# A new order for the opening of a sparse-attention and gated feed-forward kernel

## The chip, the core and the metric

The kernel runs as one program on one core of a Trainium2 chip. The time is that of the whole program on the device, in microseconds. Three runs of the kernel before gave 633.43, 633.52 and 633.88 us; the median is 633.52 us. A separate profiled execution gives the trace that is read here.

## The reference

Attention comes first. For each of 4 batches and 8 heads there are 768 positions of 64 numbers. A query sees the keys closer than 16 positions and 24 summaries of the whole sequence, one for every 32 positions: the largest key of a block (by element) with the mean of its values. Then each token's 8 heads are joined to 512 numbers and pass a feed-forward layer with a gate.

```python
block, window = (32, 16)
k_sum = k.reshape(B, H, nb, block, D).max(axis=3)
v_sum = v.reshape(B, H, nb, block, D).mean(axis=3)
scores_l = scale * np.matmul(q, k.transpose(0, 1, 3, 2))
mask_l = np.abs(pos[:, None] - pos[None, :]) < window
scores_s = scale * np.einsum('bhsd,bhnd->bhsn', q, k_sum) + np.log(block)
a = softmax over [scores_l where mask_l, scores_s]      # in words
attn = np.matmul(a, np.concatenate([v, v_sum], axis=2))
h = x @ w_in            # 3072 x 512 by 512 x 2048
return (h * np.cos(h)) @ w_out
```

## The kernel before

The 3072 tokens are cut into 8 blocks of 384. In a block the heads go in four pairs, called a, b, c and d; `a0` is pair a of block 0, `b1` pair b of block 1. The feed-forward width of 2048 is cut into 16 slices of 128 (`w0` to `w15`), and a *step* (`s0` to `s127`) is one slice of one block: four groups of three matmuls up, the gate, and nine matmuls down. Steps 0 to 5 and 22 to 31 belong to block 0, steps 6 to 21 to block 1. Each float32 operand of a step is split into a high and a low part, so three products stand for one.

Nothing is scheduled by a compiler: a table `ORDER` of 2098 short words is read from left to right, and each word records the instructions of one operation. Each engine then runs its instructions in the order in which they were recorded, and a semaphore holds an instruction back until what it reads is there. So a word that waits holds back everything behind it on its engine. A word names whose it is, what is done, and then PSUM banks or buffers and the engine: `a` is ScalarE (ACT), `v` VectorE (DVE), `p` GpSimd (POOL). The words that matter below:

- `k`, `q`, `v`, `l`: loads, all issued by SyncE's queue (SP). `v1_0.l` is the first of eight loads with block-wise V of batch 1; all eight land in one buffer, `kn` (line 246), so the next can start only when the last one is summed.
- `tk`, `tq`: TensorE turns K and Q (lines 516 and 503); `ck`, `cq` copy them out of PSUM; `ks` takes the largest key of each block (line 535); `ms` and `sc` put mask and scores into PSUM (lines 554 and 579); `mx` is the maximum (line 597), `ex` the exponential (line 614), `iv` the inverse sum (lines 624 and 627).
- `nm` multiplies the weights by it on POOL (line 630), `tp` turns them (line 639), `cp` copies them out, `va` multiplies by the values (line 683), and `xh` and `xl` write the result as high part and rest (lines 372 and 376).
- `m` copies the means of V under a pair's values, on POOL (line 372, `<-early`); in batch 0 the means come from `vm` and `ve`.
- `v1_0.s` sums such a load of V: as one reduction on DVE (line 261), or on POOL by halving (lines 251 and 267 or 270).
- A weight slice is made by `ab` and `sh` on ACT, `fb` on DVE (line 416), then `hi` and `lo` (lines 372 and 376).
- `u` is a quarter of a step's products up (line 738), `up` all of them (line 726); `tu`, `re`, `si`, `ga` the gate (the last is line 758 and frees the bank); `dh` and `dl` the products down (line 786).
- `h0.w` to `h7.w` are eight matmuls with no use for the result, put between the first operations (line 930).

The loop that reads the table (lines 1001 to 1006):

```python
    with tc.manual_schedule(engines=everything):
        prepare()
        for token in ORDER.split():
            who, what, *args = token.split(".")
            one = whose[who]
            getattr(one, does[type(one)][what])(*(int(a) if a.isdigit() else eng_of[a] for a in args))
```

Of the kernel before, what the change touches and what calls it, by code (L numbers as in the profile page):

```python
# [37 lines left out]
c1.m.p d1.ms.4.2 c0.xh.v d1.sc c0.xl d0.va.0 b1.nm d1.mx.1 b0.cp.0.a b0.cp.1.v a1.tp.0.7 w2.ab.1 c1.iv a1.tp.1.6 c1.nm
s1.u.0.3 w2.sh d0.xh.v d1.ex.3 d0.xl b0.va.1 b0.xh.v s0.u.0.5 b0.xl v1_2.s.p s0.u.2 s1.u.2 s1.u.3 a1.cp.0.v c1.tp.1.7
s1.u.1 s0.u.3 w2.fb w2.hi.v a1.cp.1.a d1.iv d1.v c1.v c1.tp.0.2 s0.u.1 s1.tu.0 w4.l.6 w5.ab.0 a1.va.4 s0.tu.1 w2.lo.v  # L40
w5.sh v1_3.l s0.re d1.nm s1.re s2.u.0.6 s2.u.2 s2.u.3 c1.cp.0.a d1.tp.1.1 c1.cp.1.v c1.va.2 d1.tp.0.0 w3.l.7 s0.si
w5.fb w5.hi.v d1.cp.1.a b1.tp.0.7 w5.lo.v s1.si s1.ga s0.ga d1.cp.0.a b1.v s2.u.1 d1.va.1 b1.tp.1.0 s5.u.0.5 a1.xh.a
c1.xh.a w8.l.0 a1.xl s1.hi.0.a s0.hi.1.a d1.xh.v d1.xl s1.lo.0.v s0.lo.1.v w4.ab.1 b1.cp.1.a w4.sh v1_3.s.v s5.u.2
s2.tu.0 s5.u.3 s2.re b1.m.p v1_4.l s5.u.1 w4.fb s0.dh.1.0.3 s2.si s0.dl s2.ga s2.hi.1.v s2.lo.1.p w3.ab.0 b1.cp.0.v
c1.xl w4.hi.a s1.dh s1.dl s2.dh s2.dl w4.lo.v b1.va.4 w3.sh s4.u.0.6 s4.u.2 w9.l.1 b1.xh.a w3.fb w3.hi.v b1.xl s4.u.3
w3.lo.p s4.u.1 w8.ab.1 s5.tu.1 w7.l.7 s6.up.4 v1_4.s.0.v s4.tu.0 s4.re w8.sh v1_5.l s4.si s5.re s3.u.0.2 s5.si w9.ab.0
w8.fb w10.l.2 s4.ga s4.hi.0.v s11.up.7 s4.lo.0.p s5.ga w9.sh s5.hi.1.a w9.fb s3.u.2 s3.u.3 s3.u.1 w8.hi.a s3.tu.0
s5.lo.1.v w9.hi.a w6.l.6 s6.tu.1 s10.up.6 w8.lo.p a2.v a2.m s3.re s6.re s5.dh s3.si s3.ga s3.hi.1.v w7.ab.1 w9.lo.v
s4.dl s3.lo.0.p s4.dh s3.dh v1_5.s.v w7.sh w10.ab.0 s3.dl s5.dl w7.fb w7.hi.v s6.si s6.ga s8.up.2 s6.hi.0.v w10.sh
s11.tu.0 s6.lo.0.v w10.fb s5.ta.0.a s10.tu.1 w10.hi.a w10.lo.p w7.lo.v s9.up.4 s11.re s10.re s5.ta.1.v s11.si s10.si  # L50
w6.ab.1 s7.up.1 s11.ga v1_6.l s10.ga w12.l.7 v1_6.s.v s10.hi.1.a w6.sh s10.lo.1.v v1_7.l s6.dh.5.7.6 w6.fb w12.ab.0
s11.hi.0.a s6.dl s11.lo.0.v w6.hi.a s5.ta.2.v s7.tu.1 s8.tu.0 s7.re s10.dh s11.dh s10.dl v1_7.s.v s11.dl w12.sh s7.si
s8.re w13.l.6 s7.ga s16.up.0 s8.si s8.ga s8.hi.1.a s15.up.1 w12.fb s7.hi.0.a s14.up.2 a2.k s5.st.0 w6.lo.v w12.hi.a
w13.ab.1 s7.lo.1.p s7.dh a2.kt.1 s15.tu.1 s5.st.1 s15.re w13.sh s5.st.2 s8.lo.0.p w12.lo.v s15.si s15.ga w15.l.7
a2.kt.0 b2.k s8.dl s8.dh w13.fb w11.l.6 s14.tu.0 s15.hi.0.a s14.re s14.si s7.dl s15.lo.0.v s16.tu.1 s15.dh s15.dl
s16.re s14.ga s14.hi.1.v s14.lo.1.p s12.up.3 w13.hi.a a2.ks.1 s16.si s16.ga a2.q s16.hi.0.a s16.lo.0.v s12.tu.0
b2.kt.0 w15.ab.0 s13.up.1 w13.lo.v w15.sh s18.up.0 s19.up.2 b2.kt.1 s13.tu.1 a2.ks.0 c2.k w15.fb b2.ks.0 w11.ab.1
w11.sh b2.ks.1 s12.re s16.dl s14.dh s12.si s13.re w11.fb s16.dh s12.ga w15.hi.a a2.qt s12.hi.1.a s14.dl w11.hi.v
s13.si s12.lo.0.v c2.kt.0 s13.ga s18.tu.0 s13.hi.0.a w14.l.6 w11.lo.p s18.re s18.si s18.ga s12.dh s18.hi.1.v s12.dl
s13.lo.1.v s19.tu.1 c2.kt.1 s18.lo.0.p s19.re d2.k s9.tu.0 s13.dh s9.re w14.ab.1 s19.si w15.lo.p s9.si w14.sh s18.dh  # L60
s18.dl s13.dl s19.ga s9.ga w14.fb s19.hi.0.a w14.hi.a a2.kw.v s9.hi.1.v s17.up.0 s23.up.3 b2.q a2.sc.2.1 w14.lo.p
b2.kw.a s19.lo.0.v d2.kt.1 d2.kt.0 a2.z.1 s19.dh a2.z.0 s19.dl a2.mx.2 s17.tu.1 s17.re s17.si s9.dh b2.qt s17.ga c2.q
s9.lo.1.v c2.ks.1 b2.sc.2.4 s17.hi.0.a b2.z.0 c2.ks.0 a2.su a2.ex.0 b2.z.1 s21.up.0 v2_0.l s21.tu.0 b2.mx.0 s17.lo.0.v
s21.re s21.si b2.su s20.up.4 a2.sm s26.up.1 c2.qt a2.iv s20.tu.1 s20.re c2.kw.a s21.ga c2.sc.0.2 a2.nm s17.dh s17.dl
s20.si d2.q v2_0.s.1.p a2.pt.0 s20.ga a2.po b2.ex.1 v2_1.l b2.sm c2.z.0 s21.hi.1.a s20.hi.0.a s20.lo.0.v s23.tu.1
b2.iv s23.re s9.dl s21.dh c2.z.1 a2.pi d2.qt s23.si s20.dl d2.ks.1 s21.lo.1.p s20.dh s21.dl d2.ks.0 s21.ta.2.0.a b2.nm
b2.pt.1 s23.ga s25.up.0 d2.kw.a s21.st.2 s25.tu.0 s23.hi.1.v s22.up.2 s23.lo.0.v s27.up.6 s21.ta.1.0.a b2.po a3.q
s22.tu.1 c2.mx.1 c2.su s25.re s22.re s30.up.7 s25.si s25.ga v2_1.s.p s21.ta.0.1.a s22.si s22.ga s22.hi.0.a s22.lo.1.p
a2.va.2 b2.pi d2.sc.5.0 s27.tu.1 s27.re d2.z.0 s22.dh.3.4.5 a3.kw.a s27.si s23.dl s23.dh s21.st.1 v2_2.l s25.hi.0.a
s25.lo.0.p d2.z.1 s25.dh s27.ga s22.dl b2.m d2.mx.2 s27.hi.1.v s25.dl a2.xh.v s27.dh b2.v s27.lo.1.p s26.tu.0 s21.st.0  # L70
s26.re s26.si s27.dl c2.ex.2 s26.ga a2.xl a3.qt s26.hi.0.a d2.su c2.sm b2.va.2 c2.m c2.iv d2.ex.3 v2_2.s.p v2_3.l
d2.sm c2.nm s24.up.6 s29.up.0 c2.v s24.tu.1 b2.xh.v s26.lo.0.p c2.pt.0 d2.iv s24.re s24.si c2.po s24.ga s24.hi.1.a
s28.up.1 s29.tu.0 s24.lo.1.v d2.nm s28.tu.1 s31.up.6 v2_3.s.v s28.re b3.q s24.dh s28.si s28.ga s26.dl s28.hi.1.a c2.pi
s29.re s24.dl d2.pt.0 s28.dh b2.xl s28.lo.0.v v2_4.l s26.dh d2.po s29.si s29.ga s29.hi.1.a c2.va.0 d2.m d2.v
s29.lo.1.v s31.tu.1 s30.tu.0 s30.re a3.sc.1.2 s30.si b3.kw.a b3.qt s30.ga c2.xh.a s30.hi.0.a a3.z.0 s31.re s31.si
s31.ga s28.dl s29.dh s29.dl s31.hi.1.a s31.lo.0.v s30.lo.1.p s30.dh s30.dl s31.dh s31.dl v2_4.s.1.v a3.z.1 a3.mx.0
c2.xl a3.su b3.sc.2.1 d2.pi d2.va.0 d2.xh.v d2.xl s32.up.6 s32.tu.1 s32.re s32.si s32.ga s32.hi.0.a v2_5.l v2_5.s.p
s31.fe.1.0 s31.ad.1 s33.up.0 s36.up.7 s34.up.4 s33.tu.0 s33.re b3.z.0 s32.lo.1.v s33.si s33.ga s33.hi.1.v a3.ex.0
s34.tu.1 s31.fe.2.1 s31.ad.2 s38.up.0 b3.z.1 b3.mx.1 v2_6.l s31.st.1 s34.re a3.sm c3.kw.a s35.up.1 s34.si s34.ga
s32.dh.2.4.5 s34.hi.0.a s32.dl s33.dh s33.lo.0.p s33.dl s34.dh c3.q s31.fe.0.0 s31.ad.0 v2_6.s.p a3.v v2_7.l  # L80
s34.lo.1.p s34.dl c3.qt s35.tu.0 s35.re s35.si s35.ga s36.tu.1 s35.hi.1.v s35.lo.0.p s35.dh s35.dl s36.re s36.si
c3.sc.1.3 s31.st.0 d3.q s31.st.2 b3.su b3.ex.1 s37.up.6 s36.ga a3.iv a3.nm a3.pt.1 c3.z.1 s36.hi.0.v v2_7.s.v d3.qt
# [954 lines left out]
```

## Time and profile before

| what | value |
|---|---|
| median of three runs | 633.52 us |
| the profiled execution | 633.6 us |
| its span, first to last instruction | 631.9 us |
| TensorE (PE) busy | 621.1 us, 98% |
| VectorE (DVE) busy | 422.1 us, 67% |
| ScalarE (ACT) busy | 323.9 us, 51% |
| GpSimd (POOL) busy | 204.6 us, 32% |

The span is 1.7 us shorter than the execution it belongs to. TensorE's granted clock is 1.00 of full speed in all 40 slices of the span. A busy PE is not a PE at its peak: matmuls overlap, and a group's recorded end lies a little after the start of the group behind it.

### The profile page before, as it was taken

The page shows a single profiled execution, that of the slowest core. Times are in us where ns is not written, and L with a number is a line of the kernel's source. Part 1 is how long each engine was busy: PE and PEld are TensorE (multiplying, and loading weights), DVE is VectorE, ACT ScalarE, POOL GpSimd, SP SyncE. Part 2 cuts the span into 40 slices and gives each one's busy share as a digit, 9 for nine tenths or more (in the row PEclk, how much of TensorE's full clock was granted, in tenths as well). Part 3 has the DMA queues.
Part 4 walks back from the last instruction along what each step waited for, and adds up shares of the span by engine and source line. Part 5 has one row for each costly group of instructions (what it writes and reads, how often), then busy time and mean ns, then how long its engine had stood idle before and what let it go on. Part 6 is the DMA issues. An engine that isn't in the chain of part 4 may idle for free.

```text
span 631.9 us, 12130 instructions
## 1 busy us (share of the span) xinstructions
PE 621.1 (98%) x4568; PEld 544.3 (86%) x4568; DVE 422.1 (67%) x814; ACT 323.9 (51%) x606; POOL 204.6 (32%) x218
## 2 busy tenths in 40 slices
...
GB/s 223 261 220 272 297 123 250 145 54 123 122 143 133 112 95 174 102 61 108 109 110 126 117 93 102 121 47 77 108 98 61 117 75 56 114 35 17 1 1 50
DMA packets 170058, 73.52 MB, mean 116 GB/s; under 512 B 136848, under 2 KB 158864, under 8 KB 170000
## 3 DMA queue, kind: packets, MB, share of 16 engines
...
q14 instruction: 22, 0.18, 0.1%
...
HBM read 54.43 MB, written 16.52 MB: 112 GB/s over the span
## 4 chain that ended last, share of the span: by engine, by line
PE 92%; DVE 4%; SPq 2%; DMA 1%; issue 1%; ACT 1%; POOL 0%; POOLq 0%; DVEq 0%
PE banks L786 41%; PE banks L726 40%; PE banks L683 3%; PE banks L567 3%; PE banks L930 1%; SPq L475 1%; DVE stage L416 1%; PE banks L738 1%; PE banks L579 1%; SPq L483 1%; PE banks L516 0%; PE banks L909 0%; DMA late<-in_v_dram 0%; DMA x<-in_v_dram 0%; DVE kd L535 0%
## 5 line engine op out<-in xcount | busy, mean ns | idle before, releaser
L726 PE MATMUL banks<-xh,w 128*128 128x384 f32 x976 | 255.5, 337 | 0.5 <-DVE t L758 0.5
L786 PE MATMUL banks<-w,gh 128*128 128x512 f32 x768 | 196.5, 392 | 0.1
L726 PEld LDWEIGHTS banks<-xh,w 128*128 128x128 f32 x976 | 176.8, 188 | 3.1 <-issue 0.8
L786 PEld LDWEIGHTS banks<-w,gh 128*128 128x128 f32 x768 | 142.6, 188 | 31.4 <-DVE gh L372 1.8
L726 PE MATMUL banks<-xl,w 128*128 128x384 f32 x488 | 163.2, 334 | 0.0
L376 POOL TENSOR_TENSOR gl<-t,gh 128x384 fp32r<-128x384 f32 x63 | 65.9, 1048 | 283.3 <-DVE gh L372 147.8
L746 ACT ACTIVATE t<-banks 128x384 int32<-128x384 f32 x128 | 62.0, 488 | 126.8 <-PE banks L726 59.7
L749 DVE SCALAR_TENSOR_TENSOR t<-t,banks 128x384 f32<-128x384 int32 x128 | 69.1, 546 | 68.3 <-ACT t L746 67.6
L786 PE MATMUL banks<-w,gl 128*128 128x512 f32 x384 | 108.0, 392 | 0.0
L754 ACT ACTIVATE t<-t 128x384 f32<-128x384 f32 x128 | 65.9, 523 | 63.4 <-DVE t L749 63.1
L726 PEld LDWEIGHTS banks<-xl,w 128*128 128x128 f32 x488 | 91.6, 188 | 0.4
L758 DVE TENSOR_TENSOR t<-t,banks 128x384 f32<-128x384 f32 x128 | 69.4, 547 | 33.1 <-ACT t L754 32.1
L786 PEld LDWEIGHTS banks<-w,gl 128*128 128x128 f32 x384 | 71.6, 188 | 15.7 <-POOL gl L376 0.5
L370 ACT CAST gh<-t 128x384 fp32r<-128x384 f32 x66 | 33.5, 511 | 43.5 <-DVE t L758 25.5
L630 POOL TENSOR_TENSOR sc<-sc,r 128x720 f32<-128x720 f32 x28 | 39.0, 1392 | 43.5 <-DVE r L627 41.0
L602 POOL TENSOR_TENSOR sc<-sc,m 128x720 f32<-128x720 f32 x24 | 34.3, 1433 | 49.6 <-DVE m L594 49.6
L376 DVE TENSOR_TENSOR gl<-t,gh 128x384 fp32r<-128x384 f32 x65 | 36.8, 569 | 12.5 <-ACT gh L370 7.5
L372 DVE CAST gh<-t 128x384 fp32r<-128x384 f32 x62 | 23.1, 373 | 18.1 <-PE banks L786 14.9
L586 DVE SCALAR_TENSOR_TENSOR sc<-banks,mask 128x360 f32<-128x360 f32 x48 | 24.5, 523 | 12.5 <-PE banks L567 12.2
L620 DVE TENSOR_REDUCE r<-sc 128x6 f32<-128x726 f32 x24 | 21.6, 902 | 13.8 <-ACT sc L609 13.8
L376 POOL TENSOR_TENSOR w<-stage,w 128x1024 fp32r<-128x1024 f32 x8 | 19.8, 2470 | 31.3 <-DVE w L372 20.0
L609 ACT ACTIVATE sc<-sc 128x720 f32<-128x720 f32 x24 | 19.4, 807 | 19.0 <-POOL sc L602 18.8
(121 smaller groups left out, 621.4 us busy)
## 6 DMA issues: line engine op xcount, KB each, us to landing
...
```

The source lines that it names most:

```text
L370: eng.copy(out=out, in_=in_)
L372: eng.tensor_copy(out=out, in_=in_)
L376: eng.tensor_tensor(out=lo, in0=src, in1=hi.bitcast(F32), op=ALU.subtract)
L586: nc.vector.scalar_tensor_tensor(out=self.sc.rearrange("p (c h) n -> p c h n", h=2)[:, :, hh, :], in0=self.sp[hh], scalar=SCALE, in1=mask[ ...
L602: nc.gpsimd.tensor_tensor(out=self.sc, in0=self.sc, in1=self.m.unsqueeze(2).broadcast_to([P, U, NK]), op=ALU.subtract)
L630: nc.gpsimd.tensor_tensor(out=self.sc, in0=self.sc, in1=self.r.unsqueeze(2).broadcast_to([P, U, NK]), op=ALU.mult)
L726: nc.tensor.matmul(out=self.h, lhsT=w_of(name, self.f)[:, c * P : (c + 1) * P], rhs=x_of(self.blk, part, c), start=n == 0, stop=n == last,)
L746: nc.scalar.activation(out=self.t.bitcast(I32), in_=self.h, func=AF.Copy, scale=1.0 / TWO_PI, bias=0.25)
L749: nc.vector.scalar_tensor_tensor(out=self.t, in0=self.t.bitcast(I32), scalar=-TWO_PI, in1=self.h, op0=ALU.mult, op1=ALU.add)
L754: nc.scalar.activation(out=self.t, in_=self.t, func=AF.Sin, scale=-1.0, bias=-0.5 * math.pi)
L758: nc.vector.tensor_tensor(out=self.t, in0=self.t, in1=self.h, op=ALU.mult)
L786: nc.tensor.matmul(out=accs[self.run][i], lhsT=g[:, i * P : (i + 1) * P], rhs=w_of(name, self.f), start=self.first and n == 0, stop=self.l ...
```

## The change

The table `ORDER` is new from its first word up to the products of block 2's first scores, some 145 us into the trace of before; from there on both tables are the same words. Both hold the same 2098 operations. Loads and stores keep their order on SP. Some of the operations use other PSUM banks, and in some the last letter is another one, so that the copy or sum runs on another engine: `v1_0.s` moves from DVE to POOL and stands far earlier, the low parts of weight slices 0, 1 and 15 (and others) move between POOL and DVE, and copies of K and Q swap between ACT and DVE. The changed file is one line shorter, so all its line numbers are one less than those of before (line 630 is 629 there).

```diff
@@ -25,152 +25,151 @@
-b1.tq.5 a0.tp.0.3 b1.cq.v b1.ms.2.6 b1.sc w0.l.7 d0.iv c0.nm b0.nm a0.m.p d0.m.p b0.m.p d1.q v1_0.s.0.v a1.ex.0 h3.w.5
...
+d0.ck.0.a a0.iv c1.q d0.ks.0 b0.ck.0.a a0.nm c0.cq.a v1_0.s.0.p d0.ks.1 c0.ms.6.7 w1.ab.0 a0.v b0.ms.3.5 d0.ck.1.v
...
```

What stands on POOL from the first normalisation on. Before (`sc` is the weights of pairs a and b, `late_108` of c and d; the copies are the means for a0 (`vn`), d0 (`x_1_115`), b0 (`early`), c0 (`x_0_114`), d1 (`late_107`) and a1 (`late_106`)):

```order
L630 TENSOR_TENSOR sc<-sc,r 128x6x120
L376 TENSOR_TENSOR w_465<-stage_381,w_465 128x1024
L630 TENSOR_TENSOR late_108<-late_108,r 128x6x120
L630 TENSOR_TENSOR sc<-sc,r 128x6x120
L372 COPY vn<-early 24x768
L372 COPY x_1_115<-early 24x768
L372 COPY early<-early 24x768
L372 COPY late_107<-early 24x768
L372 COPY x_0_114<-early 24x768
L630 TENSOR_TENSOR late_108<-late_108,r 128x6x120
L630 TENSOR_TENSOR sc<-sc,r 128x6x120
L372 COPY late_106<-early 24x768
```

The same place on POOL in the changed kernel, up to the second row on `late_108`, which is pair d of block 0:

```order
L629 TENSOR_TENSOR sc<-sc,r 128x6x120
L250 TENSOR_TENSOR kn<-kn 96x256
L250 TENSOR_TENSOR kn<-kn 96x128
L266 TENSOR_TENSOR vs_85<-kn 96x64
L629 TENSOR_TENSOR late_108<-late_108,r 128x6x120
L371 COPY vn<-early 24x768
L629 TENSOR_TENSOR sc<-sc,r 128x6x120
L371 COPY x_0_114<-early 24x768
L371 COPY late_106<-early 24x768
L371 COPY x_1_115<-early 24x768
L629 TENSOR_TENSOR late_108<-late_108,r 128x6x120
L371 COPY late_107<-early 24x768
```

The sum of the first V load (three rows on `kn`) now stands ahead of the normalisations of c0, b0 and d0 and of all copies; weight slice 1's low part (`w_465`) is gone from POOL. The order of the rest is c0, a0's means, b0, c0's and a1's means, and the normalisation of a1 (`sc`) now comes only after a second sum of a load and two more copies.

The second place is on DVE, where the results of pairs d and b of block 0 are written and weight slice 2 is made. Before:

```order
L372 CAST xh_0_708<-banks 128x384
L376 TENSOR_TENSOR xl_0_734<-banks,xh_0_708 128x384
L372 CAST xh_0_609<-banks 128x384
L376 TENSOR_TENSOR xl_0_645<-banks,xh_0_609 128x384
L372 COPY pt<-banks 120x512
L416 SCALAR_TENSOR_TENSOR stage_758<-late_109,first 128x1024
L372 CAST w_818<-stage_758 128x1024
```

In the changed kernel, where `xh_0_588` and `xl_0_594` are pair b's result, `stage_733` and `w_808` weight slice 2, and `w_702` weight slice 0:

```order
L371 CAST xh_0_700<-banks 128x384
L375 TENSOR_TENSOR w_702<-stage_662,w_702 128x1024
L375 TENSOR_TENSOR xl_0_720<-banks,xh_0_700 128x384
L596 TENSOR_REDUCE m_81<-banks 128x3 x2
L371 CAST xh_0_588<-banks 128x384
L415 SCALAR_TENSOR_TENSOR stage_733<-late_109,first 128x1024
L375 TENSOR_TENSOR xl_0_594<-banks,xh_0_588 128x384
```

The instruction that joins weight slice 2 (line 416, now 415) has moved between pair b's high part and its rest.

## Rows read from the trace of the kernel before

**Rows 1.** Busy time by stretch: stretch, its length, PE, PEld, DVE, ACT, POOL, clock, DMA, GB/s.

```profile
0.00:30.00 30.00, 27.75 (x390) 17.72 (x391) 19.20 (x64) 18.63 (x74) 16.85 (x42) 1.00 1.03 244
30.00:65.00 35.00, 31.27 (x393) 25.76 (x393) 32.29 (x57) 27.92 (x66) 23.43 (x22) 1.00 0.94 247
65.00:150.00 85.00, 85.00 (x509) 76.53 (x510) 73.11 (x124) 64.53 (x94) 31.08 (x20) 1.00 0.64 168
150.00:632.00 482.00, 477.05 (x3282) 424.30 (x3280) 297.51 (x573) 212.86 (x373) 133.22 (x135) 1.00 0.36 90
```

**Rows 2.** Timeline of PE: start, length, operation, and the wait before with its releaser.

```profile
32.53 0.52 PE L503 MATMUL banks<-ident,qn 128*128 128x128 f32 x3 [0.29 <-DMA qn<-in_q_dram]
...
36.88 0.43 PE L639 MATMUL banks<-ident,late 128*120 128x128 f32 x2 [0.73 <-ACT sc L614]
...
39.75 0.92 PE L683 MATMUL banks<-pt,x 120*64 120x64 f32 x24 [0.92 <-DVE xl L376]
40.60 0.87 PE L639 MATMUL banks<-ident,sc 128*120 128x128 f32 x6
...
46.04 0.43 PE L639 MATMUL banks<-ident,late 128*120 128x128 f32 x2 [0.91 <-POOL late L630]
...
49.19 0.91 PE L683 MATMUL banks<-pt,late 120*64 120x64 f32 x22 [0.27 <-DMA late<-in_v_dram]
...
56.10 0.44 PE L738 MATMUL banks<-xh,w 128*128 128x384 f32 x1 [0.41 <-DVE t L758]
...
67.96 0.33 PE L726 MATMUL banks<-xh,w 128*128 128x384 f32 x1
```

**Rows 3.** Timeline of SP's queue: V load for `kn`, d1's Q, next V load.

```profile
19.63 1.07 SPq L246 DMA_DIRECT2D kn<-in_v_dram  x1
...
26.10 0.91 SPq L454 DMA_DIRECT2D qn<-in_q_dram  x2
29.05 0.34 SPq L246 DMA_DIRECT2D kn<-in_v_dram  x1
```

**Rows 4.** Timeline of POOL.

```profile
26.20 1.39 POOL L630 TENSOR_TENSOR late<-late,r 128x720 f32<-128x720 f32 x1
27.54 1.39 POOL L630 TENSOR_TENSOR sc<-sc,r 128x720 f32<-128x720 f32 x1
29.00 0.82 POOL L372 COPY vn<-early 24x768 f32<-24x768 f32 x1
29.76 0.83 POOL L372 COPY x<-early 24x768 f32<-24x768 f32 x1
...
34.34 1.39 POOL L630 TENSOR_TENSOR sc<-sc,r 128x720 f32<-128x720 f32 x1
35.79 1.70 POOL L372 COPY late<-early 24x768 f32<-24x768 f32 x1
37.57 1.59 POOL L251 TENSOR_TENSOR kn<-kn 96x256 f32<-96x256 f32 x2
39.24 0.71 POOL L270 TENSOR_TENSOR vs<-vs,kn 96x64 f32<-96x64 f32 x2
...
45.94 2.59 POOL L251 TENSOR_TENSOR kn<-kn 96x256 f32<-96x256 f32 x2
```

**Rows 5.** Timeline of DVE.

```profile
21.86 1.22 DVE L416 SCALAR_TENSOR_TENSOR stage<-late,first 128x1024 int32<-128x1024 int32 x1
...
27.99 1.03 DVE L261 TENSOR_REDUCE vs<-kn 96x64 f32<-96x512 f32 x1
...
42.89 0.56 DVE L372 CAST xh<-banks 128x384 fp32r<-128x384 f32 x1 [0.43 <-PE banks L683]
43.48 0.56 DVE L376 TENSOR_TENSOR xl<-banks,xh 128x384 fp32r<-128x384 f32 x1
...
44.97 2.09 DVE L416 SCALAR_TENSOR_TENSOR stage<-late,first 128x1024 int32<-128x1024 int32 x1 [0.33 <-POOL sc L630]
```

More of the change, by code (lines that the diff above doesn't have):

```diff
@@ L38 @@
[L38 to L82, printed above, removed]
@@ new lines @@
+s24.up.6 s29.up.0 c2.v s24.tu.1 b2.xh.v s26.lo.0.p c2.pt.0 d2.iv s24.re s24.si c2.po s24.ga s24.hi.1.a s28.up.1
+s29.tu.0 s24.lo.1.v d2.nm s28.tu.1 s31.up.6 v2_3.s.v s28.re b3.q s24.dh s28.si s28.ga s26.dl s28.hi.1.a c2.pi s29.re
+s24.dl d2.pt.0 s28.dh b2.xl s28.lo.0.v v2_4.l s26.dh d2.po s29.si s29.ga s29.hi.1.a c2.va.0 d2.m d2.v s29.lo.1.v
+s31.tu.1 s30.tu.0 s30.re a3.sc.1.2 s30.si b3.kw.a b3.qt s30.ga c2.xh.a s30.hi.0.a a3.z.0 s31.re s31.si s31.ga s28.dl
+s29.dh s29.dl s31.hi.1.a s31.lo.0.v s30.lo.1.p s30.dh s30.dl s31.dh s31.dl v2_4.s.1.v a3.z.1 a3.mx.0 c2.xl a3.su
@@ new lines @@
+s31.st.2 b3.su b3.ex.1 s37.up.6 s36.ga a3.iv a3.nm a3.pt.1 c3.z.1 s36.hi.0.v v2_7.s.v d3.qt s36.lo.1.p s38.tu.0
+s37.tu.1 s37.re s38.re b3.sm s39.up.3 s40.up.7 b3.iv s37.si s38.si s36.dh s36.dl s37.ga s38.ga b3.nm s37.hi.1.a
+s37.lo.0.p s37.dh s37.dl s39.tu.1 c3.z.0 s39.re s38.hi.0.a s38.dh s38.lo.1.v s40.tu.0 s38.dl d3.kw.a d3.sc.6.0 a3.po
+b3.pt.1 s40.re s40.si s40.ga s40.hi.1.v s39.si s39.ga s39.hi.0.v s39.lo.0.p c3.mx.2 c3.su d3.z.1 a3.m a4.k a3.pi
+a3.va.3 s42.up.7 s41.up.0 s43.up.1 d3.z.0 d3.mx.0 s40.lo.1.v d3.su c3.ex.2 d3.ex.3 c3.sm s41.tu.1 a4.kt.0 a4.kt.1
```

232 lines of the change are left out of this document (133 added, 99 removed).

## The prediction

> **What bounds the kernel now.** I read the busy time by stretch first. From 65 to 150 us PE is busy 85.00 of 85.00 us, so there the end is set by PE's own work; from 30 to 65 us it is busy 31.27 of 35.00 [rows 1]. Everything that the change can win lies ahead of 65 us. Next the timeline of PE. Between 30 and 65 us it shows six waits of 0.29, 0.73, 0.92, 0.91, 0.27 and 0.41 us [rows 2], 3.53 us together, nearly all of the 3.73 us that PE is short there. They end on a load of Q, on ACT, DVE, POOL, a load of V, and DVE: no engine is the bound alone, but DVE is busy 32.29 of these 35 us [rows 1]. Last I read the queues that the change reorders, SP and POOL.
>
> Both tables hold the same matmuls, so PE's work is the same and the end moves by the change in its waits. Two landmarks make this countable: the turn of a1's weights (40.60 us) and the first products up of block 1 (67.96 us) [rows 2]. In both tables the same PE operations stand ahead of each. I sum what changes up to the first landmark, between the two, and behind the second.
>
> **Up to the first landmark: the sum of the V load on POOL.** Before, the sum of the first V load is one reduction of 1.03 us on DVE at 27.99 us [rows 5]. Now it is three rows on POOL, directly behind a0's normalisation, and everything that POOL does for PE queues behind it. It can't start before its load has landed. SP issues that load at 19.63 and is done with it at 20.70 [rows 3]; loads keep their order, so this stays. No row shows the landing: it lies between 20.70 and 27.99 us, where DVE used it without a wait. The nearest row is d1's Q: issued by 27.01 [rows 3], and PE waited for it until 32.53 [rows 2], 5.5 us later. I take 5.5 us, so 26.2. A normalisation takes 1.34 us from its start to the next one's (26.20 to 27.54) and a copy of means 0.76 (29.00 to 29.76), but a1's copy 1.70 [rows 4]. The sum of the load: its two halvings took 1.59 us once and 2.59 another time, and two of the small additions 0.71 [rows 4]; that makes 1.59 + 0.36 = 1.95 at the low end and 2.95 at the high end. I take 2.0, since the nearest row in time, at 37.57, has 1.59.
>
> POOL from 26.2 us to the end of a1's normalisation: the sum 2.0; normalisations of c0, b0, d0 and a1, 4 x 1.34 = 5.4; copies for a0, c0, d0, c1, d1 and b0, 6 x 0.77 = 4.6; a1's copy 1.7; the second sum 1.59 + 0.71 + 0.1 = 2.4. Together 16.1, so 42.3 us. Before, a1's normalisation ended at 34.34 + 1.39 = 35.73 [rows 4] and held nobody. Now PE turns a1's weights at 42.3 instead of 40.60: **1.7 us lost**. Smaller waits ahead of it on POOL (a0's means, d0's normalisation) and the three waits of 0.29, 0.73 and 0.92 us lie inside these 42.3 us and are not counted again. DVE is relieved of 1.03 us, and SP may issue the second V load when the first sum ends, at 28.2 instead of 29.05 [rows 3], so the loads behind it come some 0.8 us sooner.
>
> By the Trainium skill's "SBUF — State Buffer", section "Who interferes with whom", a DVE instruction with two inputs in SBUF and a GpSimd instruction that reads SBUF exclude each other for the whole instruction. The trace agrees as far as it goes: the join of a weight slice on line 416 took 1.22 us with POOL between two pieces of work and 2.09 us beside POOL's normalisations and sums [rows 5]. The page would set the low part of weight slice 1, which DVE now makes near 27 us, against the sum on POOL; that is the third rival below.
>
> **Between the landmarks.** Before, this is 67.96 - 40.60 = 27.36 us [rows 2] with waits of 0.91, 0.27 and 0.41, 1.59 us as recorded. A wait costs more than its record: without one, a group starts some 0.1 to 0.2 us ahead of the recorded end of the group in front. With two waits under 0.2 us that I leave without rows, I count 2.3 us in all. What becomes of them: the 0.91 us ended on c1's normalisation, which stood behind b1's and now stands directly behind a1's, at 43.6 us, while PE wants it some 2.8 us after 42.3; gone. The 0.27 us ended on a load of V that now comes 0.8 us sooner, while PE comes later; gone. The 0.41 us ended on step 0's gate, which DVE did behind all three parts of weight slice 5; now it stands behind the first part alone; gone. So **2.3 us won**.
>
> What is late next: pair b's rest now stands behind the join of weight slice 2 on DVE. From the end of b0's values on, DVE needs 0.56 for the high part, 2.09 for the join (POOL works beside it, as it did before) and 0.56 for the rest [rows 5], 3.2 us. PE has six short groups to do meanwhile, some 2.65 us, and then needs the rest: **0.55 us lost**. With the join at 1.22 us this wait would be gone. PE's products are also cut in two more places by attention's small matmuls, at an estimated 0.12 us each: **0.25 us lost**. The other moves of copies between ACT and DVE I cost at nothing here: their producers end ahead of PE's use, under products of steps 0 to 5. If that cover went, one such copy would cost its 0.56 us [rows 5].
>
> **Behind the second landmark.** PE was busy all the time up to 150 us with DVE busy 73.11 and ACT 64.53 of 85 us [rows 1], so both have over 11 us to give. I cost the new order there at 0, with 0 to 1 us as its bounds. From about 145 us on the tables are the same, and PE, without waits, carries on what it has won or lost.
>
> **Sum.** 1.7 - 2.3 + 0.55 + 0.25 = 0.2 us later. The profiled execution took 633.6 us, 0.08 above the median of 633.52, so 633.8 against it and **633.7 us** against the median: no change that can be measured. Called no change is what lies within 0.2%, 1.27 us.
>
> **Rivals.**
> 1. *The load lands sooner than I take it.* For it: only its upper bound is a row of its own; against it: the queues are busy, 1.03 of the DMA engines' capacity up to 30 us [rows 1]. Landing at 24.6 would put a1's normalisation at 40.7, the first landmark at its old place, and leave the gain between the landmarks: 633.5 - 1.5 = 632.0 us. Faster. Chance 0.22.
> 2. *The gain is given back behind the second landmark.* DVE and ACT have more work in the first 65 us than they can do without delay, and the gates of steps 3 to 6 stand behind new weight work. With 1 us of waits, 634.7 us. For it: DVE busy 92% from 30 to 65 us; against it: 11 us of room behind. Chance 0.08.
> 3. *POOL becomes the bound.* Place: POOL from the landing of the V load to a1's normalisation. Price: both sums at the slow rate, 2.59 in place of 1.59 for the halvings, 2.0 us in all, so a1's normalisation at 44.3, and 633.7 + 2.0 = 635.7 us. For it: DVE is now fuller of weight work beside POOL; against it: the sum at 37.57 had a busy DVE beside it and took 1.59 [rows 4]. It decides from where a1's normalisation ends past 43.4 us. Slower. Chance 0.2.
> That the change does nothing at all is not possible here: POOL's row order is another one.
>
> **How the numbers follow.** The forecast of a balance has 0.5, its own range 632.6 to 634.8. Faster by over 0.2%: 0.14 of the first rival, 0.06 from the forecast's lower edge, 0.20. Slower by over 0.2%: 0.18 of the third rival, 0.03 of the second, 0.05 of the forecast's upper edge, 0.26. Within: 0.54. The range for 8 in 10 reaches from the first rival to just short of the third: 631.9 to 635.5 us.
>
> **What would show it.** POOL idle from some 16.5 us to the landing near 26 us, with three rows on the V load behind it; PE waiting for POOL ahead of a0's values and of a1's turn, and that turn at 42.3 us; no wait of PE on c1's normalisation; a wait of about half a microsecond on DVE's rest of pair b; the first products up of block 1 at 68.1 us. I am wrong if that turn comes before 41 or after 43.5 us, or if PE waits again between 70 and 150 us.

## The result: 1% slower

The changed kernel took 639.73 us (median of four runs, 639.09 to 643.24) against 633.51 us. The ratio is 1.011, with a 95% interval of 1.0078 to 1.0141. Forecast was no measurable change, 633.7 us with a range of 631.9 to 635.5; what came is a clear loss of 6.2 us, above the range. The profiled execution took 643.24 us, the longest of the four. A second profile, of an execution of 640.38 us nearer to the median, is therefore shown among the experiments and used beside it.

Busy time by stretch in the changed kernel, in the columns of [rows 1]; the last two rows are two stretches of 5 us inside the second:

```profile
0.00:30.00 30.00, 25.03 (x336) 15.79 (x336) 20.33 (x65) 17.57 (x71) 15.12 (x42) 1.00 1.05 248
30.00:65.00 35.00, 31.80 (x423) 25.98 (x424) 25.65 (x48) 25.39 (x63) 19.79 (x23) 0.90 0.89 222
65.00:150.00 85.00, 81.71 (x467) 71.81 (x466) 74.82 (x113) 64.09 (x94) 26.65 (x17) 1.00 0.62 163
...
30.00:35.00 5.00, 4.52 (x47) 3.95 (x51) 2.34 (x6) 2.51 (x3) 4.78 (x6) 0.66 1.22 243
...
40.00:45.00 5.00, 5.00 (x43) 3.31 (x44) 2.81 (x7) 2.22 (x7) 4.16 (x5) 0.66 0.70 209
```

Two things differ from [rows 1]. From 65 to 150 us PE is no longer busy all the time: 3.3 of 85 us are missing. And the granted clock is not 1.00 throughout: a mean of 0.66 over 5 us is 3.4 us at 0.5, which is the lower level, 1.2 GHz. That comes twice. It is not most of the loss, though: the fastest timed run, 639.09 us, has a mean granted clock of 1.000 and is 5.6 us over the kernel before.

PE's timeline of the changed kernel, with the waits and the two landmarks (47.11 and 72.36 us, answering to 40.60 and 67.96 in [rows 2]):

```profile
30.48 1.11 PE L682 MATMUL banks<-pt,vn 120*64 120x64 f32 x24 [2.86 <-POOL vn L371]
...
39.73 0.29 PE L578 MATMUL banks<-kd,late 64*64 64x24 f32 x2 [2.43 <-issue]
...
47.11 0.65 PE L638 MATMUL banks<-ident,sc 128*120 128x128 f32 x4
...
72.36 0.34 PE L725 MATMUL banks<-xh,w 128*128 128x384 f32 x1
...
107.64 0.97 PE L785 MATMUL banks<-w,gl 128*128 128x512 f32 x3 [1.52 <-DVE gl L375]
129.35 0.96 PE L785 MATMUL banks<-w,gl 128*128 128x512 f32 x3 [0.48 <-DVE gl L375]
132.13 1.67 PE L785 MATMUL banks<-w,gh 128*128 128x512 f32 x6 [0.44 <-DVE gh L371]
137.72 0.84 PE L566 MATMUL banks<-first,qd 64*64 64x120 f32 x24 [0.44 <-ACT first L369]
```

Three stretches add up to the loss. Up to the first landmark 6.5 us are lost. Between the landmarks it takes 25.25 us instead of 27.36, 2.1 won. From the second landmark to the last products down it takes 563.46 us instead of 558.28, 5.2 lost: together 9.6, which is 643.2 - 633.6. "Issue" in the second row means that the profile shows nothing that PE waited for.

POOL in the changed kernel, answering to [rows 4]. The first two rows are the sum of the V load, then come c0's normalisation, a0's means, and last a1's normalisation:

```profile
25.31 1.25 POOL L250 TENSOR_TENSOR kn<-kn 96x256 f32<-96x256 f32 x2 [9.30 <-DMA kn<-in_v_dram]
26.64 0.32 POOL L266 TENSOR_TENSOR vs<-kn 96x64 f32<-96x64 f32 x1
27.07 2.46 POOL L629 TENSOR_TENSOR late<-late,r 128x720 f32<-128x720 f32 x1
29.60 0.82 POOL L371 COPY vn<-early 24x768 f32<-24x768 f32 x1
...
41.39 1.39 POOL L629 TENSOR_TENSOR sc<-sc,r 128x720 f32<-128x720 f32 x1
```

POOL idles 9.30 us for the load, as forecast, and a1's normalisation ends at 42.78 us (forecast 42.3). So the end of that chain was right, but in part by luck: the load landed 0.9 us sooner than taken (25.31 against 26.2), and the row behind it took 17.5 us instead of 16.1. The largest single excess is c0's normalisation, 2.46 us instead of 1.39. DVE made the low part of weight slice 1 at the same moment. Here is that row, and below it the same row of DVE and a0's means on POOL in the second profile, where c0's normalisation started 0.08 us ahead of it, at 27.55 us:

```profile
27.07 1.22 DVE L375 TENSOR_TENSOR w<-stage,w 128x1024 fp32r<-128x1024 f32 x1
```

```profile
27.63 2.38 DVE L375 TENSOR_TENSOR w<-stage,w 128x1024 fp32r<-128x1024 f32 x1
29.00 1.70 POOL L371 COPY vn<-early 24x768 f32<-24x768 f32 x1
```

There DVE's part took 2.38 us instead of 1.22, and then the copy of a0's means 1.70 instead of 0.82. Either way PE gets a0's means some 1 us later. PE's turn of a1's weights came 4.3 us behind the end of a1's normalisation in the first profile.

Behind the second landmark, here are three DVE instructions of the changed kernel and, below, the POOL instructions beside them:

```profile
99.60 1.88 DVE L269 TENSOR_TENSOR vs<-vs,part_sum 96x64 f32<-96x64 f32 x1
...
104.62 2.04 DVE L415 SCALAR_TENSOR_TENSOR stage<-late,first 128x1024 int32<-128x1024 int32 x1 [0.21 <-ACT first L408]
...
127.95 1.35 DVE L375 TENSOR_TENSOR gl<-t,gh 128x384 fp32r<-128x384 f32 x1
```

```profile
98.99 2.41 POOL L375 TENSOR_TENSOR w<-stage,w 128x1024 fp32r<-128x1024 f32 x1
104.55 1.02 POOL L375 TENSOR_TENSOR gl<-t,gh 128x384 fp32r<-128x384 f32 x1 [3.15 <-DVE gh L371]
...
126.35 2.54 POOL L375 TENSOR_TENSOR w<-stage,w 128x1024 fp32r<-128x1024 f32 x1
```

An addition of 96x64 takes 1.88 us and ends at 101.48, 0.08 us behind POOL's low part of slice 6 (101.40). The low part of step 12 takes 1.35 us in place of 0.56 and ends 0.41 us behind POOL's low part of slice 11. The join of slice 12 takes 2.04 in place of 1.21 us and ends 1.09 us behind POOL's low part of step 7. Each ends behind POOL's by its own undisturbed time (0.22, 0.56 and 1.21 us) less 0.12 to 0.15 us, so these DVE instructions seem to get nowhere until POOL's is about to end. The waits at 107.64 and 129.35 us are for the low parts of steps 8 and 12, which stand behind them.

### The profile page after: what moved, and what is told of

It reads as the page before. It is cut to its first block, busy times and chain, and to the rows that moved or that the text cites. A ratio compares the mean times of both kernels' runs of the same rounds, so it can differ in the third digit from the quotient of the medians.

```text
span 641.5 us, 12139 instructions
## 1 busy us (share of the span) xinstructions
PE 625.2 (97%) x4568; PEld 545.7 (85%) x4568; DVE 425.4 (66%) x811; ACT 326.8 (51%) x608; POOL 199.2 (31%) x221
## 4 chain that ended last, share of the span: by engine, by line
PE 86%; DVE 5%; DMA 2%; ACT 2%; SPq 1%; issue 1%; POOL 1%; DVEq 0%; POOLq 0%; ACTq 0%
PE banks L785 38%; PE banks L725 36%; PE banks L682 4%; PE banks L566 3%; PE banks L737 2%; DVE stage L415 2%; DMA kn<-in_v_dram 2%; SPq L453 1%; PE banks L638 1%; DMA late<-in_q_dram 1%; ACT first L408 1%; PE banks L578 1%; DVE part_sum L260 0%; DVE t L748 0%; PE banks L929 0%
## 5 line engine op out<-in xcount | busy, mean ns | idle before, releaser
L375 POOL TENSOR_TENSOR gl<-t,gh 128x384 fp32r<-128x384 f32 x66 | 69.0, 1046 | 293.0 <-DVE gh L371 147.3
L369 ACT CAST gh<-t 128x384 fp32r<-128x384 f32 x63 | 31.9, 511 | 42.8 <-DVE t L757 24.2
L371 DVE CAST gh<-t 128x384 fp32r<-128x384 f32 x65 | 25.6, 393 | 17.7 <-PE banks L785 14.3
L652 DVE STREAM_TRANSPOSE stage<-sc 128x768 f32<-128x768 f32 x24 | 23.3, 973 | 7.3 <-POOL sc L629 7.2
```

Source lines behind the costliest of these rows:

```text
L369: eng.copy(out=out, in_=in_)
L371: eng.tensor_copy(out=out, in_=in_)
L375: eng.tensor_tensor(out=lo, in0=src, in1=hi.bitcast(F32), op=ALU.subtract)
```

## The experiments

Theory A: up to the first landmark POOL's row is what PE waits for, and the clock fall behind the wait adds to it. Theory B: behind the second landmark POOL's low parts hold up DVE's instructions. In all, the kernels gave these landmarks in their profiles (us; "behind" is from the first products up of block 1 to the last products down) and these medians of timed runs:

| kernel | a0's values | turn of a1 | products up | behind | median |
|---|---|---|---|---|---|
| before | 30.91 | 40.60 | 67.96 | 558.28 | 633.5 |
| changed | 30.48 | 47.11 | 72.36 | 563.46 | 639.73 |
| changed, again | 30.75 | 43.78 | 69.53 | 563.40 | 641.14 |
| 1 V sum on DVE | 27.73 | 42.51 | 69.22 | 563.30 | 640.21 |
| 2 three low parts on DVE | 30.79 | 44.70 | 70.26 | 560.37 | 639.80 |
| 3 both | 28.14 | 42.92 | 69.63 | 562.02 | 636.98 |
| 4 filler ahead of a0's values | 30.48 | 43.59 | 70.31 | 563.55 | 640.61 |
| 5 as 1, a1's normalisation early | 27.46 | 40.60 | 66.47 | 563.51 | 637.74 |
| 6 as 1, filler ahead of the turn | 27.54 | 43.66 | 68.85 | 563.41 | 638.99 |
| 7 before's order from 68 us on | 30.45 | 42.89 | 68.36 | 560.72 | 637.06 |
| 8 before, V sum on POOL | 31.31 | 41.25 | 69.90 | 558.26 | 635.54 |
| 9 as 5, four low parts on DVE | 28.65 | 41.80 | 68.17 | 561.12 | 636.15 |
| 10 as 5, before's order from 68 us on | 27.84 | 40.28 | 68.56 | 560.58 | 636.53 |
| 12 before, two moves on POOL | 30.75 | 39.58 | 67.79 | 558.19 | 633.43 |

**The changed kernel again.** No edit.

> The changed kernel once more, for a profile nearer to its median (the profiled execution shown took 643.2 us, the median was 639.7). Theory A: PE's wait of some 2.9 us at a0's values and the clock fall at 31 us are there again; where PE's stall without a releaser is shorter than 2.4 us or absent, PE waits for a1's normalisation instead, and turns a1's weights at 42.8 to 45 us, never before POOL's row lets it; behind the first products up of block 1 it takes 563.3 to 563.7 us as in all kernels with that order. Rival (the stall is part of the change's order and always the same): the turn comes at 47 us again.

Measured: 641.14 us (639.67 to 643.70), ratio 1.0127 (1.0103 to 1.0151). PE's timeline in the second profile:

```profile
30.75 0.92 PE L682 MATMUL banks<-pt,vn 120*64 120x64 f32 x24 [2.58 <-POOL vn L371]
38.03 0.29 PE L578 MATMUL banks<-kd,late 64*64 64x24 f32 x2 [2.06 <-issue]
43.78 0.65 PE L638 MATMUL banks<-ident,sc 128*120 128x128 f32 x4
```

The wait and the stall are there again, and the turn comes at 43.78. PE did not wait for a1's normalisation, which had ended at 43.08. But the clock stays at 1.00 in all stretches, behind a wait of 2.58 us: the fall that theory A expected does not come every time. Nearer to the median, then, the loss is 3.2 us up to the first landmark, 1.6 won between, 5.1 lost behind.

**1. The V sum back on DVE.**

```diff
-a0.nm c0.cq.a v1_0.s.0.p d0.ks.1
+a0.nm c0.cq.a d0.ks.1
-a0.m.p b0.iv b0.nm
+a0.m.p b0.iv a0.cp.1.v a0.cp.0.v v1_0.s.0.v v1_1.l c0.v d0.v w2.l.6 b0.v b0.nm
```

The five loads that stood behind the sum move with it, and two copies of a0's turned weights.

> The changed kernel with the first V sum back on DVE, so that no load stands ahead of c0's normalisation on POOL. Theory A (the sum on POOL makes PE idle 2.9 us, the granted clock then falls to half for 3.4 us, and both together are most of the 6.5 us lost up to the turn of a1's weights): a0's values start by 28.5 us instead of 30.5, the granted clock stays at 1.00 up to 36 us, the turn of a1's weights comes at 41 to 43 us instead of 47.1, and the time is 634 to 636.5 us. Rival (PE's stall of 2.4 us without any wait, and the clock fall behind it at 41 us, come from the order of the matmuls and stand by themselves): the second clock fall stays, the turn comes at 44 us or later, the time is 637 us or more. Both expect the losses behind 72 us to stay (some 5 us in the profiled run).

Measured: 640.21 us (638.81 to 640.77), so no gain, and neither forecast held in full. PE and POOL:

```profile
42.51 0.65 PE L638 MATMUL banks<-ident,sc 128*120 128x128 f32 x4 [2.28 <-POOL sc L629]
```

```profile
27.47 3.21 POOL L629 TENSOR_TENSOR sc<-sc,r 128x720 f32<-128x720 f32 x1
...
40.21 2.25 POOL L629 TENSOR_TENSOR sc<-sc,r 128x720 f32<-128x720 f32 x1
```

a0's values start 2.75 us sooner, and the first clock fall is gone, as theory A has it. But PE then arrives early at the turn of a1's weights and waits 2.28 us for a1's normalisation, which ends no sooner than in the changed kernel: two normalisations took 3.21 and 2.25 us instead of 1.39, so POOL lost again what the sum had cost it. The clock fell behind this wait. So it is POOL's whole row, not the sum in it, that sets the turn here.

**5. a1's normalisation early on POOL** (added to 1).

```diff
-d0.nm c1.m.p v1_1.s.p v1_2.l b1.cq.a w5.l.1 a0.va.6 d1.m.p ... b0.m.p ... a0.xh.v a1.iv ... a1.nm
+d0.nm b1.cq.a a0.va.6 w1.lo.v c1.tq.7 a0.xh.v a1.iv a1.nm c1.m.p v1_1.s.p v1_2.l w5.l.1 d1.m.p a1.v b0.m.p
```

> The kernel with the first V sum on DVE (the run where PE waited 2.28 us for a1's normalisation, until 42.51 us, and the clock fell behind it) and one more move on POOL: a1's normalisation stands directly behind d0's, ahead of c1's means, the second V sum and the means of d1 and b0. Theory A (up to the first landmark POOL's row is the bound, and the clock falls because PE waits for it): a1's normalisation ends by 37 us, PE turns a1's weights at 40.2 us without a wait, the clock stays at 1.00 from 40 to 50 us, the first products up of block 1 come at 65 to 66 us instead of 69.2, and the time is some 4 us under the run without the move, 635.5 to 637 us. Rival (the second sum and the copies of means are then late themselves, or the clock falls anyway): the wait reappears at b0's values or at a1's values, the first products up come at 68 us or later, the time is 638.5 us or more.

Measured: 637.74 us (637.37 to 639.29), ratio 1.0068 (1.0056 to 1.0080). POOL and PE:

```profile
34.27 2.37 POOL L629 TENSOR_TENSOR sc<-sc,r 128x720 f32<-128x720 f32 x1
```

```profile
34.85 0.29 PE L578 MATMUL banks<-kd,late 64*64 64x24 f32 x2 [1.30 <-issue]
40.60 0.65 PE L638 MATMUL banks<-ident,sc 128*120 128x128 f32 x4
```

The turn has no wait and comes at 40.60, where it was before the change, although a stall of 1.30 us stands ahead of it. No clock fall. The first products up come 1.5 us sooner than in the kernel before. Theory A holds for the waits and the clock; the size was missed, with the first products up at 66.47 us instead of 65 to 66, and 2.5 us gained on kernel 1 instead of some 4. The whole rest of the loss (637.74 against 633.46) now lies behind the second landmark, 563.51 against 558.28 us.

**4 and 6. Useless matmuls in PE's waits.** In 4 they stand ahead of a0's values in the changed kernel, in 6 ahead of the turn of a1's weights in kernel 1.

```diff
-b1.tq.5 ... a0.va.6
+b1.tq.5 ... h3.w.0 h3.w.0 h3.w.0 a0.va.6
```

```diff
-d1.sc w0.lo.v w2.sh a1.tp.0.6
+d1.sc w0.lo.v w2.sh h3.w.0 h3.w.0 h3.w.0 a1.tp.0.6
```

> The changed kernel with three matmuls of no use (h3.w again) ahead of a0's values, so that PE works for some 2.6 us in what was a wait for POOL; the sum stays on POOL. If the fall of the granted clock at 31 us follows from PE's idle time ahead of it: the clock stays at 1.00 from 30 to 35 us, and the time falls by 1.5 to 3 us against the changed kernel although PE still can't start a0's values before 30.5 us. If the clock has nothing to do with that idle time, or the lost time is the wait alone: the clock falls as before, and the time is the same within 0.7 us. The second fall, at 41 us behind a stall without a wait, is left alone by this edit; if it is a follower of the first, it goes too.

> The kernel with the first V sum on DVE, and three matmuls of no use (h3.w again) ahead of the turn of a1's weights, where PE waited 2.28 us for POOL. This prices the clock fall by itself. If the fall follows from PE's idle time: the turn still comes at 42.5 us, the clock stays at 1.00 from 43 to 48 us, the first products up of block 1 come some 1.7 us sooner (67.5 instead of 69.2 us), and the time falls by 1 to 2 us. If the fall has another cause it stays, and the time is the same or longer.

Measured: 640.61 us (639.05 to 641.35) for 4, 638.99 us (637.24 to 639.64) for 6. The clock by stretch, first of kernel 4, then of kernel 1 and of kernel 6:

```profile
31.00:35.00 4.00, 4.00 (x99) 3.35 (x97) 2.85 (x8) 2.98 (x4) 3.85 (x5) 1.00 1.06 199
...
44.00:48.00 4.00, 4.00 (x36) 3.45 (x35) 0.55 (x2) 0.55 (x2) 2.66 (x5) 0.57 1.19 273
```

```profile
43.00:48.00 5.00, 5.00 (x42) 4.41 (x41) 2.00 (x3) 3.17 (x11) 2.57 (x5) 0.66 1.05 216
```

```profile
43.00:48.00 5.00, 5.00 (x49) 4.12 (x48) 2.69 (x6) 2.11 (x10) 2.57 (x5) 1.00 1.06 211
```

In 4 the fall at 31 us is gone, and the time is the same, not 1.5 to 3 us less: PE reaches the turn at 41.3 us, waits 2.28 us for a1's normalisation, and the clock falls behind that wait. It also gives PE's own work between a0's values and the turn, at full clock and without waits: 41.31 - 30.48 = 10.8 us.

In 6 the clock stays at 1.00, and the time is 1.2 us under kernel 1 (forecast 1 to 2), with ranges that overlap. But that isn't the filler's work, for 6 is not kernel 1 with its wait filled. Here is PE's filler, and a1's normalisation on POOL:

```profile
40.98 2.84 PE L929 MATMUL banks<-ident 128*128 128x512 f32 x6
```

```profile
40.08 1.39 POOL L629 TENSOR_TENSOR sc<-sc,r 128x720 f32<-128x720 f32 x1
```

PE met a stall of 1.53 us ahead of this, and a1's normalisation took 1.39 us instead of 2.25. So it ended at 41.47 us, and without the filler PE would have waited only 0.5 us. The filler itself put the turn at 43.66 (forecast 42.5). The price of a fall can be read all the same: from the turn to the first products down takes 11.34 us, against 12.87 in kernel 1, so a fall of 3.4 us costs some 1.5 us (in the two profiles of the changed kernel, without a fall there, it took 11.40 and 11.92).

In both pairs what differed was PE's idle time ahead of the fall. In the profiles seven falls came ahead of 60 us, each with an idle time of 2.28 to 2.86 us next to it; but the changed kernel's second profile has one of 2.58 us without a fall and without any filler. So that the falls follow from PE's idle time is likely and not shown.

**2 and 3. Low parts on DVE.** 2 has this edit on the changed kernel, 3 on kernel 1.

```diff
-w12.sh w6.lo.p s7.hi.0.v
+w12.sh w6.lo.v s7.hi.0.v
-s12.lo.0.v w11.lo.p s18.tu.0
+s12.lo.0.v w11.lo.v s18.tu.0
-w15.lo.v s19.lo.0.p b2.kw.a
+w15.lo.v s19.lo.0.v b2.kw.a
```

> The changed kernel with three low parts of weight slices and steps (slice 6, slice 11 and step 19's first half) on DVE instead of POOL. Theory B (behind 72 us PE waits because POOL's low parts stretch DVE's instructions with two inputs beside them): the sum of the V load at 98.5 us takes 1.6 instead of 3.2 us, the waits of PE at 107.6 (1.52 us) and from 129 to 138 us (0.48, 0.44, 0.44) go, the stretch from the first products up of block 1 to block 2's start takes 2 to 4 us less, and the time is 636 to 638 us. Rival (DVE simply has too much to do there, whoever stands beside it): the three parts add some 4 us of work to DVE, the waits stay or grow, and the time is 640 us or more. The loss up to 47 us stays under both.

> Both edits of the two runs before in one kernel. If the two losses are independent, its time is that of the changed kernel less the sum of the two gains: 631 to 634 us by theories A and B together, about the kernel before. By their rivals 637 us or more.

Measured: 639.80 us (636.98 to 642.35) and 636.98 us (634.96 to 639.05). In the profile of 2 the stretch behind the second landmark takes 560.37 us, 3.1 less, as theory B has it; two waits of PE are left, 0.17 and 0.96 us. The median doesn't show it: three of its six runs took 637 to 638 us and three over 641, so it lies between the two forecasts. The three over 641 us have a mean granted clock of 0.993 or 0.994, the others 0.997 to 1.000. The opening of this kernel differs from run to run, so a gain of 3 us is clear only in the profile. DVE and POOL in kernel 2:

```profile
97.47 0.22 DVE L269 TENSOR_TENSOR vs<-vs,part_sum 96x64 f32<-96x64 f32 x1
...
102.59 1.17 DVE L371 CAST gh<-t 128x384 fp32r<-128x384 f32 x1
```

```profile
101.68 1.86 POOL L375 TENSOR_TENSOR gl<-t,gh 128x384 fp32r<-128x384 f32 x1 [4.82 <-DVE gh L371]
```

The addition that took 1.88 us takes 0.22 once slice 6's low part is off POOL. The wait that is left has the same look: step 8's high part takes 1.17 us (0.35 in the changed kernel) and ends at 103.76, 0.22 us behind POOL's low part of step 7. 3 gains 3.2 us on kernel 1, but behind the second landmark only 1.3 in its profile; a new wait of 1.29 us stands at 128.48 us there. Its forecast of 631 to 634 us was missed; 636.98 is at the edge of the rivals' range.

**9. Four low parts on DVE, on kernel 5.** As 2, and also:

```diff
-s7.lo.1.p
+s7.lo.1.v
-s12.lo.0.v w11.lo.v s18.tu.0 ... s18.lo.0.v s19.si
+s12.lo.0.v s18.tu.0 ... s18.lo.0.v w11.lo.v s19.si
```

> The kernel with the first V sum on DVE and a1's normalisation early, and also four low parts on DVE instead of POOL: slices 6 and 11, the first half of step 19, and step 7 (whose low part on POOL held step 8's high part on DVE until it ended); slice 11's low part stands behind step 18's. By theories A and B together: the first products up of block 1 at 66 to 67 us, PE without a wait over 0.5 us between 75 and 150 us, 559 to 560.5 us from there to the last products down, and 632.5 to 635 us, no slower than the kernel before by more than can be measured. Rival (DVE becomes the bound with four low parts more): waits of PE on DVE grow at other places, 561.5 us or more for that stretch, 637 us or more.

Measured: 636.15 us (635.43 to 637.39), ratio 1.0041 (1.0029 to 1.0054), with 561.12 us behind: missed, between the two forecasts. The wait for step 8 shrinks from 1.55 to 0.16 us, as expected. But slice 11's low part, now later on DVE, holds the buffer that slice 14 needs, ACT waits 2.00 us for it, and PE 1.36 us at block 2's first scores, where it had 0.43.

**7 and 10. Before's order behind the second landmark.** 7 has the changed kernel's words up to step 6's products up and then what is left of the words of before; 10 does so with kernel 5. In 7 the low part of step 5 reads a buffer that step 3 has overwritten, so that step's share of block 0 isn't the reference's; all instructions run.

```diff
-s6.up.5 ... (the changed table)
+s6.up.4 v1_4.s.0.v w8.sh v1_5.l s4.si s3.u.0.2 ... (the table before, without what has been done)
```

> The changed table up to the first products up of block 1, and from there on what is left in the order, on the banks and on the engines of the table before (the head's banks are renumbered to fit). It tells whether what was lost behind the second landmark comes from the order there. Theory B (it does: POOL's low parts stand beside DVE's two-input instructions and stretch them): from the first products up of block 1 to the last products down it takes 558.3 to 559.5 us as in the kernel before, instead of 563.3 to 563.6, PE has no wait over 0.3 us between 75 and 150 us, and the time is 633.5 to 636.5 us. Rival (DVE, ACT or the loads come out of the first 70 us too late, and any order would pay for it): this stretch still takes 561.5 us or more, and the time is 638 us or more.

> The head of the kernel with the first V sum on DVE and a1's normalisation early, and behind the first products up of block 1 the order of the table before (steps 4 and 5 use the other t buffer than in the first splice). In the first splice the stretch behind took 560.7 us, of which 1.6 us were waits at 81 to 83 us that came from one DVE instruction held 2.5 us by POOL's low part of slice 8. If that collision is one of timing, it can go with the earlier head: 558.5 to 560.5 us behind, the first products up at 66 to 67 us, the time 632 to 635 us. Rival (DVE and ACT come out of the head with the same lag whatever stands on POOL): the stretch takes 560.7 us again, and the time is 635 us or more.

Measured: 637.06 us (636.31 to 638.78) and 636.53 us (635.50 to 636.65). Behind the second landmark it takes 560.72 and 560.58 us: 2.7 to 2.9 us less than with the changed order, but 2.4 and 2.3 more than in the kernel before, between the two forecasts for 7 and on the rival's side for 10. DVE, POOL and PE in 7:

```profile
76.45 2.51 DVE L375 TENSOR_TENSOR gl<-t,gh 128x384 fp32r<-128x384 f32 x1 [0.17 <-ACT t L745]
```

```profile
76.11 2.43 POOL L375 TENSOR_TENSOR w<-stage,w 128x1024 fp32r<-128x1024 f32 x1 [0.92 <-ACT w L369]
```

```profile
81.20 1.66 PE L785 MATMUL banks<-w,gh 128*128 128x512 f32 x6 [0.91 <-DVE gh L371]
```

Step 5's low part, 0.56 us elsewhere, takes 2.51 and ends 0.42 us behind POOL's low part of slice 8. Both instructions stand in the same order in the kernel before, where DVE's came 0.15 us ahead of POOL's and took 0.55 us, and POOL's took 2.68 instead of 2.43:

```profile
74.45 0.55 DVE L376 TENSOR_TENSOR gl<-t,gh 128x384 fp32r<-128x384 f32 x1
```

```profile
74.60 2.68 POOL L376 TENSOR_TENSOR w<-stage,w 128x1024 fp32r<-128x1024 f32 x1 [1.34 <-ACT w L370]
```

So who comes first decides who is held. From step 12's low products on, the stretch takes 504.92 us, as before (504.93).

**8. The kernel before with the V sum on POOL.**

```diff
-d0.iv c0.nm b0.nm a0.m.p d0.m.p b0.m.p d1.q v1_0.s.0.v
+d0.iv v1_0.s.0.p c0.nm b0.nm a0.m.p d0.m.p b0.m.p d1.q
```

> The kernel before with one edit: the first V sum on POOL, ahead of c0's normalisation, instead of on DVE. Theory A says that the sum alone is cheap where POOL's row is not the bound: the four normalisations and six copies come some 1.7 us later, a0's values at 31.5 to 32.5 us instead of 30.91, a1's normalisation ends at 37.5 us, still ahead of PE's turn of a1's weights (40.6 us before); the time is 633.2 to 635 us. Rival (the sum on POOL by itself makes PE idle and the clock fall): a wait of 1 us or more at a0's values, a granted clock under 1.00 in 30 to 40 us, the time is 636 us or more.

Measured: 635.54 us (635.46 to 635.82), ratio 1.0031 (1.0020 to 1.0042). PE:

```profile
31.31 0.92 PE L682 MATMUL banks<-pt,vn 120*64 120x64 f32 x24 [0.50 <-POOL vn L371]
35.87 0.66 PE L638 MATMUL banks<-ident,late 128*120 128x128 f32 x4 [1.09 <-POOL late L629]
...
47.60 0.43 PE L638 MATMUL banks<-ident,late 128*120 128x128 f32 x2 [1.70 <-POOL late L629]
50.97 1.23 PE L682 MATMUL banks<-pt,late 120*64 120x64 f32 x24 [0.93 <-DMA late<-in_v_dram]
```

2.1 us lost, 0.5 us above the forecast, without a clock fall: about the sum's own time (1.65 us). Two waits of [rows 2] have grown (0.91 to 1.70, 0.27 to 0.93), and 0.50 and 1.09 us on POOL are new. Also in the old order POOL's row has no slack, and the sum moves everything behind it.

**12. Two moves on POOL in the kernel before.**

```diff
-d0.nm c0.v a1.iv a1.nm a1.m.p ... v1_1.s.p w2.l.6 ... b1.nm d1.mx.1 ... c1.nm s1.u.0.3
+d0.nm c0.v a1.iv v1_1.s.p a1.nm a1.m.p ... w2.l.6 ... d1.mx.1 ... c1.nm b1.nm s1.u.0.3
```

> The kernel before with two moves on POOL alone: the second V sum stands ahead of a1's normalisation instead of behind a1's means (so the loads queued behind its buffer, a1's V among them, are issued some 3 us sooner), and c1's normalisation ahead of b1's. Theory A (up to 65 us PE waits for what POOL does too late, and only the order of POOL's row matters): PE's waits of 0.91 us on c1's normalisation and 0.27 us on a1's V go, no new wait over 0.3 us comes ahead of 40.6 us since a1's normalisation still ends by 38.5 us, the clock stays at 1.00, and the time is 0.5 to 1.3 us under the kernel before, 632.2 to 633.0 us. Rival (PE then waits for the next late thing, DVE's gate of step 0 or a1's normalisation): the time is 633.2 us or more.

Measured: 633.43 us (633.33 to 634.75), ratio 0.9996 (0.9987 to 1.0005): no difference. PE:

```profile
36.72 0.43 PE L638 MATMUL banks<-ident,late 128*120 128x128 f32 x2 [0.94 <-ACT sc L613]
39.58 0.87 PE L638 MATMUL banks<-ident,sc 128*120 128x128 f32 x6
44.52 0.44 PE L638 MATMUL banks<-ident,late 128*120 128x128 f32 x2 [0.24 <-POOL late L629]
46.73 0.65 PE L638 MATMUL banks<-ident,late 128*120 128x128 f32 x4 [0.72 <-ACT late L613]
```

The rival was right. The turn comes 1.0 us sooner and the wait on c1's normalisation falls from 0.91 to 0.24 us; then PE waits 0.72 us for ACT instead, and the first products up come only 0.17 us sooner. No version tried is faster than the kernel before.

## Why the prediction was wrong

- **Up to the first landmark, forecast 1.7 us lost, measured 6.5 and 3.2.** The end of POOL's chain was right, 42.78 against 42.3 us, by terms that offset each other. What failed is "smaller waits ahead of it on POOL (...) lie inside these 42.3 us and are not counted again". PE was held until 30.5 us for a0's means, and from there it has 10.8 us of its own work to the turn (kernel 4): 41.3 us at best, only 1.5 us ahead of POOL, and what PE meets on the way beyond these adds to the end. It met a stall of 2.1 to 2.4 us, and in the profiled execution two clock falls of 1.5 us (kernel 6). 41.3 + 2.4 + 3.0 = 46.7, measured 47.1. Of the second profile 30.75 + 10.8 + 2.06 gives 43.6, measured 43.78. Where the same opening met one clock fall and no stall (kernel 7), PE came early enough to wait 0.27 us for POOL, and the turn was at 42.89, near the forecast. The prediction has no term for the stall or the clock.
- **The third rival** did not come as priced: a1's normalisation ended at 42.8 and 43.1 us, not past 43.4. The collision that stands behind it did come, one instruction later than named: slice 1's low part met c0's normalisation, not the sum. And its mechanism, POOL as the bound, was at work: PE waited for it at a0's values, where PE came early to the turn it waited 2.28 us there (kernels 1, 3 and 4), and with a1's normalisation moved up the loss in this stretch was gone (kernel 5).
- **Between the landmarks**, forecast 1.5 us won net (2.3 less 0.55 and 0.25), measured 2.1 and 1.6. Right. The three waits are gone, and that for pair b's rest didn't appear: the join of weight slice 2 took 1.22 us in both profiles, the case for which the prediction said that this wait would be gone. Its 0.55 us rested on the 2.09 us of a join that POOL held.
- **Behind the second landmark**, "I cost the new order there at 0, with 0 to 1 us as its bounds" is the step that failed most: 5.1 to 5.2 us in both profiles, and 563.3 to 563.6 us for the stretch in all kernels with that order. The 11 us that DVE had free over 85 us were taken for cover. A share of busy time does not tell which DVE instruction stands beside which POOL instruction. Low parts moved from POOL to DVE took back 3.1, 1.3 and 2.4 us (kernels 2, 3 and 9), the order of before 2.7 to 2.9 (7 and 10); the collisions that were left look the same.
- The rule that the prediction weighed, in the Trainium skill's "SBUF — State Buffer", section "Who interferes with whom", bears on this: DVE with two inputs in SBUF and a GpSimd instruction that reads SBUF exclude each other, as do GpSimd and DVE in a mode that takes both ports; the first holds a port pair for the whole instruction, and the later one waits. The trace agrees: DVE's held instructions end 0.08 to 0.42 us, or a join 1.09 us, behind the end of POOL's, and POOL's is held where DVE's came first (2.68 us in the kernel before). The prediction used the rule for one place ahead of the first landmark and for none of the thirteen low parts on POOL between 75 and 141 us (nine in the kernel before).
- **Left open:** the 2.0 to 2.8 us still lost behind the second landmark in kernels 2, 7, 9 and 10 are only in part tied to single collisions. The six waits of the changed kernel there are 3.3 us as recorded for 5.2 lost; the other 1.9 us is recorded busy time of PE (560.6 against 558.7 us up to the last product down). It shrinks where the waits do, to 0.9 and 0.8 us in kernels 2 and 7, so it looks like overlap lost at the waits, which no run took apart. Nor was the stall under "issue" taken apart.
